# Combine weights in later slots, dispatched sums behind the last scores, another order of the last pairs, and the output rests of two batches in one transfer

## The chip, the cores and the metric

One core of a Trainium2 chip runs the kernel. Its engines work side by side: TensorE (PE; its weight loads are shown apart as PEld), VectorE (DVE), ScalarE (ACT), GpSimd (POOL), and SyncE (SP), which here only issues DMA transfers. Sixteen DMA engines move data between HBM and the on-chip memory. The metric is the device time of one execution in microseconds; the median of three runs before the change is 213.12 us.

## The reference

Inputs are `q`, `k`, `v` of shape [8 batches, 8 heads, 576, 64], and `phi` [512, 32], `w1` [8, 512, 1024], `w2` [8, 1024, 512].

```python
scores = (1/8) * q @ k.T                       # per batch and head
scores = where((i - j >= 0) & (i - j < 64), scores, -1e9)
attn   = softmax(scores) @ v                   # -> x: [4608, 512]
logits = x @ phi                               # [4608, 32]
d = softmax(logits, over the 4608 rows)        # dispatch
slot_input = d.T @ x                           # 32 slots, 4 for each of 8 experts
slot_out[e] = relu(slot_input[e] @ w1[e]) @ w2[e]
c = softmax(logits, over the 32 slots)         # combine weights
out = c @ slot_out                             # [4608, 512] in fp32
```

The dispatch softmax runs over all rows, so no output row can be made before the last row of x is known.

## The kernel before

Work goes by pairs of heads: 8 batches x 4 pairs = 32 pairs. The loop `for n in range(-1, NP)` (L492) is a software pipeline written out by hand: slot `n` issues stages of several pairs, and each engine runs its instructions in the order written. In slot n, PE transposes q of pair n and k of pair n+1 (L250), ScalarE copies them (`qb` L262, `kT` L257); PE computes the masked scores of pair n-1 for the row maxima (`st_max`, L273 and L276, in `a_m`), VectorE takes the maxima (L278, L289); PE computes the scores of pair n-2 (L299, L301; blocks 0 to 7 in `a_s`, the last block in `a_k`), ScalarE the exponentials (`pt`, L306, and L312 for the last block); PE multiplies pair n-3 with v (L323, in `a_v`), VectorE normalises it (L332, L333, into `x_b`); PE transposes pair n-4 (L347) and ScalarE copies it (`xt`, L351). L293 and L294 bring the maxima into the score matmul of the next pair.

Once for every batch, that is in every fourth slot each, stages of the mixture follow, with lags from the batch's first pair: at lag 8 the logits (`fr_logits`, L361, copied by ScalarE to `lg`, L366), at lag 9 the running maximum (`fr_max`, L371 and L373, `nmax`), its exponential (`fr_exp`, L387 and L388, `d` and `al`) and a 32x32 turn of the logits (`fr_turn`, L378, `lgT`), at lag 10 the dispatch (`fr_dispatch`, L433 and L434, copied to `dT`, L438 and L439) and the dispatched sums (`fr_slots`, L445 and L448, in `a_m`; added up by VectorE in `fr_acc`, L457). The combine weights are made at lag 11 (`cb_max`, L399), lag 12 (`cb_sub` on GpSimd L404, `cb_exp` on ScalarE L410, `cb_sum` on VectorE L416 and L417), lag 13 (`cb_mul` on GpSimd, L424) and lag 15 (`cb_turn` on VectorE, L429, into `ct_all`). The tiles `lg` and `ec` share one tag with two buffers.

GpSimd issues all loads of q, k, v and of the expert weights in `loads(n)` at the head of a slot. `w` are seven experts' weights, 1 MB a transfer; the eighth expert's come in quarters (`w1h` L125, `w2h` L131) into buffers of q and k. The last load is the fourth `w1h`, issued at L569 (`loads(NP)`).

Behind the loop L568 to L658 write out the last pairs and the last batch: the last scores, normalisations, transposes and logits, the merge of the maxima (`mg`), the dispatched sums, the normalised slot input `sit` (L643, L647). `fill(k)` issues k matmuls whose results nobody reads. Then `first` (L682) and `second` (L702) compute the experts with all 32 slots in four column groups, `osb` and `so4` carry the slot outputs, and the output loop (L730) makes for each batch 576 rows: 128-row blocks in pieces of one or two, and a rest of 64 rows. PE multiplies (L738), ScalarE and VectorE take turns to copy a piece to `ob` (four buffers of 5 x 512), and SyncE issues one transfer per piece (L748), 25 in all. Eight completion semaphores are used in turn for the transfers, so the issue of one waits for the one eight before it.

Of the kernel before, what the change touches and what calls it, by code (L numbers as in the profile page):

```python
# [9 lines left out]
FP32 = mybir.dt.float32  # L10
# [8 lines left out]
def kernel(  # L19
# [10 lines left out]
    nc = tc.nc  # L30
# [432 lines left out]
    def of(n, lag):  # L463
        b, r = divmod(n - lag, HP)
        return b if r == 0 and 0 <= b < B else None
# [26 lines left out]
    for n in range(-1, NP):  # L492
        loads(n)
        lb, eb, sb, cb = [of(n, lag) for lag in range(8, 12)]
        if of(n, 12) is not None:
            cb_sub(of(n, 12), nc.gpsimd)
        if of(n, 13) is not None:
            cb_mul(of(n, 13), nc.gpsimd)

        if live(n - 1):  # L500
            st_max(n - 1)
            st_max8(n - 1)
        if live(n - 3):
            st_av(n - 3)
        if live(n - 1):
            st_max8_read(n - 1)
        if live(n - 3):
            st_norm(n - 3)

        if live(n):  # L510
            st_transpose(n, "qs", a_qh)
            st_copy_q(n)

        if sb is not None:
            fr_dispatch(sb)
# [12 lines left out]
        if live(n + 1):  # L528
            st_transpose(n + 1, "ks", a_kh)
        if live(n - 2):  # L530
            st_exp8(n - 2)
        if live(n + 1):
            st_copy_k(n + 1)
        if eb is not None:
            fr_exp(eb)

        if lb is not None:
            fr_logits(lb)
        if live(n - 4):
# [23 lines left out]
    def fill(k):  # L563
        for _ in range(k):
            nc.tensor.matmul(a_k[:, :], ident_h[:, :], wm[:, 0:4, :].rearrange("p c x -> p (c x)"),
                             start=True, stop=True, skip_group_check=True)

    b, p = B - 1, NP - 1  # L568
# [22 lines left out]
    nc.vector.memset(a_s[:, 0, 128:192], -1.0e30)  # L591
# [6 lines left out]
    st_av(p)  # L598
    fr_stat(b - 1)
    st_norm(p)  # L600
# [5 lines left out]
    fr_dispatch_copy(b - 1, th, nc.vector.tensor_copy)  # L606
# [47 lines left out]
    cb_max(b)  # L654
    cb_sub(b, nc.vector)
    cb_sum(b - 1)
    cb_mul(b - 1, nc.vector)
    cb_turn(b - 1)  # L658
    pmid.close()
    patt.close()  # L660
    pex = ExitStack()
    psh = pex.enter_context(tc.tile_pool(name="psh", bufs=6, space=bass.MemoryType.PSUM))
# [3 lines left out]
        t = psh.tile([128, 512], FP32, name=name, tag="ph")  # L666
        return t, t[:, :].bitcast(FP16)

    ptl = ctx.enter_context(tc.tile_pool(name="ptl", bufs=1))
    pou = ctx.enter_context(tc.tile_pool(name="pou", bufs=4))  # L670


    so_ps = pso.tile([128, D], FP32, name="so_ps")
    op = pso.tile([128, D], FP32, name="op")
    hs = [ptl.tile([128, F], FP16, name=f"hs{g}") for g in range(2)]
    hT = [ptl.tile([128, NFC, 128], FP16, name=f"hT{g}") for g in range(2)]

    def first(g, f2):
        ha, _ = bank("ha")
# [19 lines left out]
    def second(g, fcs):  # L699
        for fc in fcs:  # L700
            for j in range(4):
# [17 lines left out]
    osb = ptl.tile([128, D], FP16, name="osb")  # L719
    nc.scalar.copy(out=osb, in_=op[:, :])  # L720
    nc.tensor.matmul(so_ps[:, :], ss[:, :, :].rearrange("p t s -> p (t s)"), osb[:, :], start=True, stop=True,
                     skip_group_check=True)
    so4 = ptl.tile([128, D], FP16, name="so4")
    nc.vector.tensor_copy(out=so4, in_=so_ps)
    pex.close()
    pst = ctx.enter_context(tc.tile_pool(name="pst", bufs=4, space=bass.MemoryType.PSUM))


    turn = 0
    for b in range(B):  # L730
        ob = pou.tile([128, 5, D], FP32, name="ob", tag="ob")
        for ts in ((0,), (1,), (2, 3), (4,)) if b == 0 else ((0, 1), (2, 3), (4,)):
            cp = pst.tile([128, 2, 512], FP32, name="cp", tag="cp")
            for i, t in enumerate(ts):
                pn = 128 if t < 4 else 64
                r = slice(32 * t, 32 * t + 32) if t < 4 else slice(96, 128)
                o = 0 if t < 4 else 128
                nc.tensor.matmul(cp[0:pn, i, :], ct_all[r, b, o:o + pn], so4[r, :], start=True, stop=True,  # L738
                                 skip_group_check=True)
            t0, nt = ts[0], len(ts)  # L740
            dst, src = ob[0:pn, t0:t0 + nt, :], cp[0:pn, 0:nt, :]
# [5 lines left out]
            r0 = 576 * b + 128 * t0  # L747
            nc.sync.dma_start(out=out[r0:r0 + pn * nt, :].rearrange("(c p) d -> p c d", p=pn), in_=dst)  # L748
# [1 line left out]
_INS = ['q', 'k', 'v', 'moe_phi', 'moe_w1', 'moe_w2']  # L750
_OUTS = [((4608, 512), 'float32')]
# [25 lines left out]
```

## Time and profile before

| | |
|---|---|
| median of 3 runs | 213.12 us (212.01 to 214.09) |
| the profiled execution | 211.88 us, its span 209.9 us |
| PE, DVE, ACT, POOL busy | 79%, 67%, 67%, 48% of the span |
| loop of 32 slots | to about 150 us |
| last pairs to `sit` | 150 to 168 us |
| experts (L682 to L724) | 168.3 to 179.1 us |
| output: first issue, last issue ended, end of span | 180.25, 205.27, 209.9 us |
| loads (q0) / output and phi (q1) | 30.94 MB / 9.50 MB |
| transfers of the output | 15 of 512 KB, 2 of 256 KB, 8 of 128 KB |

The span is the profiled stretch on the core; the execution's time includes 1.95 us around it. A line of the timeline gives start and length in us, engine, source line, operation, the tile written and the tiles read, the shape, and in brackets how long the engine was idle just before and what ended that. A DMA row gives the mean busy share of the 16 engines in tenths for each of 40 equal slices, and below it the rate in GB/s.

### The profile page before, as it was taken

How to read it: one execution, taken by the hardware profiler on the slowest of the kernel's cores; microseconds unless marked ns; L12 is line 12 of the kernel's file. 1: busy time of each engine (PE TensorE's matmuls, PEld its weight loads, DVE VectorE, ACT ScalarE, POOL GpSimd, SP SyncE). 2: the span in 40 equal slices, each digit the busy share in tenths (PEclk: the TensorE clock that was granted, in tenths of full speed). 3: DMA queues.
4: the chain of work that ended last, by engine and by line, in shares of the span. 5: the costliest groups of instructions: out<-in, count | busy, mean ns of one | idle time of the engine just before them, and what ended most of it. 6: DMA issues, size and time to landing. Idle time of an engine off the chain costs nothing.

```text
span 209.9 us, 6705 instructions
## 1 busy us (share of the span) xinstructions
PE 165.9 (79%) x2884; PEld 115.8 (55%) x2884; DVE 140.2 (67%) x332; ACT 140.0 (67%) x253; POOL 101.5 (48%) x122
## 2 busy tenths in 40 slices
PE   0696899998997999899899979989886898685000
PEld 0475677776776677577668857766673343211000
DVE  6888757667659685876869496677757574865200
ACT  2466687888888789878877987887665242744200
POOL 7969559284866476476828546653920000000000
PEclk9999999999999999999999999999999789955555
DMA  5999999999999999999999999999999910599996
GB/s 73 178 181 199 207 181 201 193 204 191 187 209 187 211 185 192 207 189 204 185 195 196 191 197 120 159 199 135 177 207 210 207 27 3 186 327 367 356 347 215
DMA packets 68124, 40.85 MB, mean 195 GB/s; under 512 B 38912, under 2 KB 59392, under 8 KB 68096
## 3 DMA queue, kind: packets, MB, share of 16 engines
q0 software_dynamic: 62560, 30.94, 111.3%
q1 hardware_dynamic: 5536, 9.50, 13.2%
q8 instruction: 22, 0.36, 0.6%
q14 instruction: 6, 0.05, 0.1%
HBM read 61.93 MB, written 9.44 MB: 340 GB/s over the span
## 4 chain that ended last, share of the span: by engine, by line
ACT 33%; PE 31%; DVE 18%; DMA 7%; issue 5%; SPq 0%; ACTq 0%; POOL 0%; DVEq 0%; POOLq 0%
ACT qb L262 10%; ACT pt L306 9%; DVE m L278 7%; DMA out_dram<-ob 4%; ACT xt L351 4%; PE a_m L273 4%; ACT kT L257 4%; PE a_q L250 4%; DVE x_b L333 4%; PE a_m L276 4%; ACT ob L743 3%; DMA qs<-in_q_dram 3%; PE ha L682 2%; PE a_v L323 2%; PE op L702 2%
## 5 line engine op out<-in xcount | busy, mean ns | idle before, releaser
L262 ACT ACTIVATE qb<-a_q 64x576 f16<-64x576 f16 x64 | 41.3, 645 | 22.5 <-PE a_q L250 22.0
L278 DVE TENSOR_REDUCE m<-a_m 128x8 f16<-128x1024 f32 x32 | 39.2, 1224 | 10.3 <-PE a_m L276 9.7
L306 ACT ACTIVATE pt<-a_s 128x1024 f16<-128x1024 f32 x32 | 32.8, 1024 | 3.1 <-PE a_s L301 2.3
L333 DVE TENSOR_TENSOR x_b<-a_v,rc 128x640 f16<-128x640 f32 x31 | 25.6, 824 | 1.1
L257 ACT ACTIVATE kT<-a_k 128x576 f16<-128x576 f16 x32 | 20.9, 654 | 5.0 <-PE a_k L250 5.0
L276 PEld LDWEIGHTS <-qb 128*128 128x128 f16 x256 | 17.1, 99 | 8.4 <-ACT qb L262 1.3
L79 POOL DMA_DIRECT2D ks<-in_k_dram x16 | 11.1, 692 | 20.9 <-PE a_k L250 18.1
L147 POOL DMA_DIRECT2D v<-in_v_dram x16 | 19.9, 1241 | 2.5 <-DMA ks<-in_k_dram 2.1
L351 ACT COPY xt<-a_q 128x576 f16<-128x576 f16 x31 | 20.2, 651 | 0.8 <-PE a_q L347 0.8
L276 PE MATMUL a_m<-kT,qb 128*128 128x128 f16 x256 | 20.0, 222 | 0.0
L250 PE MATMUL a_k<-ident_h,ks 96*64 96x96 f16 x384 | 15.0, 217 | 6.3 <-DMA ks<-in_k_dram 6.3
L299 PE MATMUL a_s<-rt,lh 128*128 128x128 f16 x256 | 19.8, 220 | 0.1
L273 PE MATMUL a_m<-wm,ident_h 128*128 128x512 f16 x64 | 19.8, 392 | 0.0
L154 POOL COPY v<-v 64x1152 f16<-64x1152 f16 x16 | 18.3, 1142 | 2.6 <-DMA v<-in_v_dram 2.0
L301 PE MATMUL a_s<-qb,kT 128*128 128x128 f16 x256 | 19.5, 219 | 0.0
L294 DVE CAST rt<-a_v 9x128 f16<-9x128 f32 x31 | 9.0, 289 | 15.8 <-PE a_v L293 15.6
L299 PEld LDWEIGHTS <-lh 128*128 128x128 f16 x288 | 17.6, 98 | 3.3 <-issue 1.6
L301 PEld LDWEIGHTS <-kT 128*128 128x128 f16 x288 | 18.8, 98 | 0.0
L156 POOL COPY v<-v 64x1088 f16<-64x1088 f16 (+1 forms) x16 | 17.9, 1117 | 0.8
L250 PE MATMUL a_q<-ident_h,qs 96*64 96x96 f16 x384 | 15.0, 212 | 3.3 <-ACT xt L351 0.9
L743 ACT COPY ob<-cp 128x1024 f32<-128x1024 f32 (+2 forms) x13 | 10.5, 848 | 8.6 <-DMA out_dram<-ob 6.5
L323 PE MATMUL a_v<-v,pt 128*64 128x65 f16 x558 | 15.7, 197 | 0.6 <-ACT pt L306 0.6
(144 smaller groups left out, 305.8 us busy)
## 6 DMA issues: line engine op xcount, KB each, us to landing
w<-in_moe_w_dram POOLq DMA_DIRECT2D x14, 1024.0 KB, 15.6
out_dram<-ob SPq DMA_DIRECT2D x15, 512.0 KB, 4.6
ks<-in_k_dram POOLq DMA_DIRECT2D x16, 288.0 KB, 12.6
qs<-in_q_dram POOLq DMA_DIRECT2D x16, 288.0 KB, 14.1
v<-in_v_dram POOLq DMA_DIRECT2D x16, 288.0 KB, 13.8
w2h<-in_moe_w_dram POOLq DMA_DIRECT2D x4, 256.0 KB, 7.2
w1h<-in_moe_w_dram POOLq DMA_DIRECT2D x4, 256.0 KB, 10.8
out_dram<-ob SPq DMA_DIRECT2D x8, 128.0 KB, 4.5
```

The lines of the kernel that those rows point to most:

```text
L147: nc.gpsimd.dma_start(out=v1s[b % 2][:, c, 0:Dh], in_=v[b].rearrange("h s d -> (h s) d").rearrange("(c p) d -> p c d", p=128)[:, c, :])
L250: nc.tensor.transpose(tq[64 * hf:64 * hf + 64, RP * r:RP * r + RP], src[0:RP, h + hf, Dh * r:Dh * r + Dh], ident_h[0:RP, 0:RP])
L257: nc.scalar.activation(kTs[p % NK][:, 64:64 + S], turned(a_kh), AF.Copy, scale=QKS)
L262: nc.scalar.activation(qbs[p % NQ][h, :, hf, :], turned(a_qh)[h], AF.Copy, scale=QKS)
L273: nc.tensor.matmul(a_m[:, j, :], ident_h[:, :], wm[:, j:j + 4, :].rearrange("p c x -> p (c x)"), start=True, stop=False, skip_group_check= ...
L276: nc.tensor.matmul(a_m[:, i // 4, 128 * (i % 4):128 * (i % 4) + 128], qblock(p, i), kwindow(p, i), start=False, stop=True, skip_group_chec ...
L278: nc.vector.reduce_max(m[:, 0:8].rearrange("p (l c) -> p l c", l=2), a_m[:, :, :].rearrange("p l (c x) -> p l c x", x=128), axis=AXX)
L299: nc.tensor.matmul(at(i), lh[:, i, :], rt[:, :], start=(i % 4 == 0), stop=False, skip_group_check=True)
L301: nc.tensor.matmul(at(i), kwindow(p, i), qblock(p, i), start=False, stop=True, skip_group_check=True)
L306: nc.scalar.activation(pt[:, 0:8, :].rearrange("p i x -> p (i x)"), a_s[:, :, :], AF.Exp, scale=XS)
L333: nc.vector.tensor_tensor(out=xbs[b][:, :, 128 * hp:128 * hp + 128].rearrange("p c (l d) -> p l c d", l=2), in0=avv[:, :, :, 0:64], in1=rc ...
L351: nc.scalar.copy(out=xts[b][:, hp, :], in_=a_qh[:, 0:S])
```

## The change

Four things are changed.

1. In the loop `cb_mul` goes from lag 13 to 17, `cb_exp` from 12 to 15, `cb_sum` from 12 to 16 and `cb_turn` from 15 to 19; `cb_sub` stays at 12.
2. In the loop the last block's scores (`st_scores(n - 2, (8,), ...)`) stand ahead of the dispatched sums `fr_acc(sb, fr_slots(sb))`.
3. Behind the loop, the maximum and the turn of batch 6 (`fr_max`, `fr_turn`) stand ahead of the normalisation of the last pairs, and the memset of `a_s` between these; the combine steps of the last batches are spread differently, most of them behind the experts' last VectorE operation; `fill` takes the bank it writes, and there are 4, 2, 5 and 2 of them (3, 2, 1, 4 and 1 before); the dispatched sums of the last batch stand ahead of the matmul that sums `ws`; `hs`, `hT`, `osb` use buffers of earlier tiles; `so4` is copied by ScalarE.
4. The output goes by two batches: four pieces of 128-row blocks (five for the first two batches) and one rest piece, in which 64 rows of each of two batches lie under each other on 128 partitions and go out in one transfer. `ob` has ten buffers of 2 x 512. There are 21 transfers. The sums, multiply and turn of the last batch stand ahead of the second two batches' pieces.

The core of the diff:

```diff
@@ the loop
-        if of(n, 13) is not None:
-            cb_mul(of(n, 13), nc.gpsimd)
+        if of(n, 17) is not None:
+            cb_mul(of(n, 17), nc.gpsimd)
...
+        if live(n - 2):
+            st_scores(n - 2, (8,), lambda i: s8)
         if sb is not None:
             fr_acc(sb, fr_slots(sb))
-        if live(n - 2):
-            st_scores(n - 2, (8,), lambda i: s8)
...
-        if of(n, 12) is not None:
-            cb_exp(of(n, 12))
+        if of(n, 15) is not None:
+            cb_exp(of(n, 15))
...
-        if of(n, 12) is not None:
-            cb_sum(of(n, 12))
-        if of(n, 15) is not None:
-            cb_turn(of(n, 15))
+        if of(n, 16) is not None:
+            cb_sum(of(n, 16))
+        if of(n, 19) is not None:
+            cb_turn(of(n, 19))
@@ behind the loop
-    cb_exp(b - 2)
-    cb_sum(b - 2)
-    cb_mul(b - 2, nc.gpsimd)
     st_score(p)
     st_scores(p, (8,), lambda i: s8)
     st_exp8(p)
+    fr_max(b - 1)
+    fr_turn(b - 1)
+    st_av(p - 1, a_m)
+    st_norm(p - 1, a_m)
     nc.vector.memset(a_s[:, 0, 128:192], -1.0e30)
-    st_av(p - 1, a_m)
-    fr_max(b - 1)
-    st_norm(p - 1, a_m)
...
     fr_transpose_copy(p, a_kh)
+    cb_sum(b - 3)
+    cb_mul(b - 3, nc.gpsimd)
...
-    fill(3)
+    fill(4, a_k[:, :])
...
-    fill(2)
...
     fr_dispatch_copy(b)
+    fill(2, a_m[:, 1, :])
...
-    fill(1)
+    fr_acc(b, fr_slots(b, a_v[:, 0, :]))
     nc.tensor.matmul(mg[:, 4:5], ssf_, ws[:, :], start=True, stop=True, skip_group_check=True)
-    fr_acc(b, fr_slots(b, a_v[:, 0, :]))
-    fill(4)
+    fill(5, a_m[:, 1, :])
...
-    fill(1)
+    fill(2, a_m[:, 1, :])
...
-    cb_turn(b - 2)
-    fr_turn(b - 1)
-    cb_max(b - 1)
-    cb_sub(b - 1, nc.vector)
-    cb_exp(b - 1)
     fr_turn(b)
     cb_max(b)
     cb_sub(b, nc.vector)
-    cb_sum(b - 1)
-    cb_mul(b - 1, nc.vector)
-    cb_turn(b - 1)
-    pmid.close()
+    cb_exp(b - 2)
...
     cb_exp(b)
-    cb_sum(b)
-    cb_mul(b, nc.vector)
-    cb_turn(b)
+    cb_max(b - 1)
+    cb_sub(b - 1, nc.vector)
+    cb_sum(b - 2)
+    cb_mul(b - 2, nc.vector)
+    cb_exp(b - 1)
+    cb_turn(b - 3)
+    cb_turn(b - 2)
+    cb_sum(b - 1)
+    cb_mul(b - 1, nc.vector)
+    cb_turn(b - 1)
     second(1, range(8))
...
-    nc.vector.tensor_copy(out=so4, in_=so_ps)
+    nc.scalar.copy(out=so4, in_=so_ps)
@@ the output
-    for b in range(B):
-        ob = pou.tile([128, 5, D], FP32, name="ob", tag="ob")
-        for ts in ((0,), (1,), (2, 3), (4,)) if b == 0 else ((0, 1), (2, 3), (4,)):
+    for b in range(0, B, 2):
+        pieces = [(b + i, ts) for i in range(2) for ts in ((0, 1), (2, 3))] + [(b, (4,))]
+        if b == 0:
+            pieces[0:1] = [(0, (0,)), (0, (1,))]
+        if b == 2:
+            cb_sum(B - 1)
+            cb_mul(B - 1, nc.vector)
+            cb_turn(B - 1)
+        for b_, ts in pieces:
...
+                    for j in range(2):
+                        nc.tensor.matmul(cp[64 * j:64 * j + 64, i, :], ct_all[96:128, b_ + j, 128:192],
+                                         so4[96:128, :], start=True, stop=True, skip_group_check=True)
...
+            if t0 < 4:
+                nc.sync.dma_start(out=out[r0:r0 + 128 * nt, :].rearrange("(c p) d -> p c d", p=128), in_=dst)
+            else:
+                nc.sync.dma_start(out=out[S * b_:S * b_ + 2 * S, :].rearrange("(t s) d -> t s d", t=2)[:, 512:S, :],
+                                  in_=ob[:, 0, :])
```

More of the change, by code (lines that the diff above doesn't have):

```diff
@@ L556, with fill @@
             cb_max(cb)
-        if of(n, 12) is not None:
-            cb_sum(of(n, 12))
-        if of(n, 15) is not None:
-            cb_turn(of(n, 15))
-    def fill(k):
+        if of(n, 16) is not None:
+            cb_sum(of(n, 16))
+        if of(n, 19) is not None:
+            cb_turn(of(n, 19))
+    def fill(k, bank):
         for _ in range(k):
-            nc.tensor.matmul(a_k[:, :], ident_h[:, :], wm[:, 0:4, :].rearrange("p c x -> p (c x)"),
+            nc.tensor.matmul(bank, ident_h[:, :], wm[:, 0:4, :].rearrange("p c x -> p (c x)"),
                              start=True, stop=True, skip_group_check=True)
@@ L598 @@
     st_av(p)
+    st_norm(p)
     fr_stat(b - 1)
-    st_norm(p)
     fr_transpose(p - 1)
@@ L605 @@
     fr_dispatch(b - 1, th)
-    fr_dispatch_copy(b - 1, th, nc.vector.tensor_copy)
+    fr_dispatch_copy(b - 1, th)
     fr_transpose(p, a_kh)
     fr_transpose_copy(p, a_kh)
+    cb_sum(b - 3)
+    cb_mul(b - 3, nc.gpsimd)
     fr_acc(b - 1, fr_slots(b - 1))
@@ L667, in bank @@
         return t, t[:, :].bitcast(FP16)
-    ptl = ctx.enter_context(tc.tile_pool(name="ptl", bufs=1))
-    pou = ctx.enter_context(tc.tile_pool(name="pou", bufs=4))
     so_ps = pso.tile([128, D], FP32, name="so_ps")
     op = pso.tile([128, D], FP32, name="op")
-    hs = [ptl.tile([128, F], FP16, name=f"hs{g}") for g in range(2)]
-    hT = [ptl.tile([128, NFC, 128], FP16, name=f"hT{g}") for g in range(2)]
+    hs_ = pxb.tile([128, 2, F], FP16, name="hs", tag="x_b")
+    hT_ = pxb.tile([128, 2, NFC, 128], FP16, name="hT", tag="x_b")
+    hs, hT = [hs_[:, g, :] for g in range(2)], [hT_[:, g, :, :] for g in range(2)]
     def first(g, f2):
@@ L714 @@
     cb_exp(b)
-    cb_sum(b)
-    cb_mul(b, nc.vector)
-    cb_turn(b)
+    cb_max(b - 1)
[8 more added lines that the diff above has]
+    cb_turn(b - 1)
     second(1, range(8))
-    osb = ptl.tile([128, D], FP16, name="osb")
+    osb = kTs[0][:, 0:D]
     nc.scalar.copy(out=osb, in_=op[:, :])
@@ L722 @@
                      skip_group_check=True)
+    pmid.close()
+    ptl = ctx.enter_context(tc.tile_pool(name="ptl", bufs=1))
+    pou = ctx.enter_context(tc.tile_pool(name="pou", bufs=10))
     so4 = ptl.tile([128, D], FP16, name="so4")
-    nc.vector.tensor_copy(out=so4, in_=so_ps)
+    nc.scalar.copy(out=so4, in_=so_ps)
     pex.close()
@@ L729 @@
     turn = 0
-    for b in range(B):
-        ob = pou.tile([128, 5, D], FP32, name="ob", tag="ob")
-        for ts in ((0,), (1,), (2, 3), (4,)) if b == 0 else ((0, 1), (2, 3), (4,)):
+    for b in range(0, B, 2):
[7 more added lines that the diff above has]
+        for b_, ts in pieces:
             cp = pst.tile([128, 2, 512], FP32, name="cp", tag="cp")
+            ob = pou.tile([128, 2, D], FP32, name="ob", tag="ob")
             for i, t in enumerate(ts):
[L735 to L739, printed above, removed]
+                if t < 4:
+                    r = slice(32 * t, 32 * t + 32)
+                    nc.tensor.matmul(cp[:, i, :], ct_all[r, b_, 0:128], so4[r, :], start=True, stop=True,
+                                     skip_group_check=True)
+                else:
+                    for j in range(2):
+                        nc.tensor.matmul(cp[64 * j:64 * j + 64, i, :], ct_all[96:128, b_ + j, 128:192],
+                                         so4[96:128, :], start=True, stop=True, skip_group_check=True)
             t0, nt = ts[0], len(ts)
-            dst, src = ob[0:pn, t0:t0 + nt, :], cp[0:pn, 0:nt, :]
+            dst, src = ob[:, 0:nt, :], cp[:, 0:nt, :]
             if turn % 2 == 0:
@@ L746 @@
             turn += 1
-            r0 = 576 * b + 128 * t0
-            nc.sync.dma_start(out=out[r0:r0 + pn * nt, :].rearrange("(c p) d -> p c d", p=pn), in_=dst)
+            r0 = S * b_ + 128 * t0
+            if t0 < 4:
+                nc.sync.dma_start(out=out[r0:r0 + 128 * nt, :].rearrange("(c p) d -> p c d", p=128), in_=dst)
+            else:
+                nc.sync.dma_start(out=out[S * b_:S * b_ + 2 * S, :].rearrange("(t s) d -> t s d", t=2)[:, 512:S, :],
+                                  in_=ob[:, 0, :])
 _INS = ['q', 'k', 'v', 'moe_phi', 'moe_w1', 'moe_w2']
```

## The prediction

> **What bounds the kernel now.** I read the page's slices first, then the output stage by its DMA rates, then the loop and the way out of it by the timeline.
>
> ```profile
> DMA  5999999999999999999999999999999910599996
> GB/s 73 178 181 199 207 181 201 193 204 191 187 209 187 211 185 192 207 189 204 185 195 196 191 197 120 159 199 135 177 207 210 207 27 3 186 327 367 356 347 215
> ```
>
> Each slice is 5.25 us. Loads fill the DMA engines to slice 31, apart from slices 24, 25 and 27, which miss (80 + 41 + 65 GB/s) x 5.25 us = 0.98 MB of a 200 GB/s rate: 4.8 us of loading. From 178 us the output fills them again. The DMA view of 180 to 209 us alone, in slices of 0.725 us:
>
> ```profile
> DMA  0499998999999999999999999999999999999920
> GB/s 0 181 367 381 384 263 201 401 404 393 271 333 404 401 348 274 401 404 393 266 328 407 401 356 268 390 404 390 288 328 390 401 376 243 384 398 404 299 93 0
> ...
> q1 hardware_dynamic: 5008, 9.44, 94.3%
> ```
>
> The engines never idle, so this stage lasts as long as its bytes take. Full rate is about 395 GB/s, 24.7 per engine: a row of 2,048 bytes takes 83 ns. Eight times the rate falls to 200 to 290 with the engines still busy: these are the eight rests, 64 rows from 64 partitions each. The stage is 4,608 rows / 16 engines = 288 rows x 83 ns = 23.9 us, plus eight rests at about half rate, 8 x 0.33 = 2.6 us: 26.5 us, against about 27.2 seen (181.1 to 208.3).
>
> The loop, one batch of four slots (18.8 us), from the timeline:
>
> ```profile
> 107.24 0.40 PE L445 MATMUL a_m<-x_b,dT 128*32 128x512 f16 x4 [0.24 <-DVE dT L438]
> ...
> 108.59 0.28 ACT L312 ACTIVATE pt<-a_k 128x128 f16<-128x128 f32 x1 [0.49 <-PE a_k L250]
> ...
> 110.92 1.30 ACT L262 ACTIVATE qb<-a_q 64x576 f16<-64x576 f16 x2 [0.98 <-PE a_q L250]
> ...
> 118.71 0.41 ACT L410 ACTIVATE ec<-lgT 128x192 f32<-128x192 f32 x1
> ...
> 119.15 0.35 DVE L416 TENSOR_REDUCE rs<-ec 128x6 f32<-128x192 f32 x1 [1.35 <-ACT ec L410]
> ...
> 119.76 1.23 DVE L278 TENSOR_REDUCE m<-a_m 128x8 f16<-128x1024 f32 x1
> ...
> 122.22 0.22 PE L293 MATMUL a_v<-ident_h,m 128*9 128x128 f16 x1 [0.99 <-DVE x_b L333]
> ...
> 122.77 0.46 ACT L387 ACTIVATE d<-lg,nmax 128x192 f16<-128x192 f32 x1 [0.31 <-DVE nmax L373]
> ```
>
> VectorE waits 1.35 us for the combine exponential; the row maxima (L278) queue behind it, then the normalisation, PE's L293 and nmax. The way out of the loop, and the last load:
>
> ```profile
> 149.79 0.58 POOL L125 DMA_DIRECT2D w1h<-in_moe_w_dram  x1
> ...
> 157.20 0.11 DVE L591 MEMSET a_s<- 128x64 f32 x1 [0.46 <-ACT pt L306]
> ...
> 159.21 0.82 DVE L333 TENSOR_TENSOR x_b<-a_v,rc 128x640 f16<-128x640 f32 x1
> ...
> 165.89 0.75 DVE L457 SCALAR_TENSOR_TENSOR acc<-acc,al,a_v 128x512 f32<-128x512 f32 x1 [1.12 <-PE a_v L448]
> ```
>
> That w1h landing is the slowest of its kind, 20.4 us: 170.2. Its matmul (L682) starts at 171.09, so the load is 0.9 us from being the bound.
>
> **The change, part by part.** Times in the frame of the 211.88 us execution (span 209.9).
>
> *Combine weights later (loop).* In its new slot the exponential stands behind xt, where ACT waits 0.53 us for PE's q transposes before qb (115.04) and the exponential takes 0.41: hidden. Its old place was such a gap too (xt 118.18, qb 119.39, both 1.2 us apart as in a slot without it), so ACT gains nothing directly. VectorE does the sums at about 117.85 without a wait, L278 starts when its matmuls end (118.5 instead of 119.76), nmax is ready at 121.45, and d follows kT at 122.34, not 122.77: 0.43 us less until the next qb. The multiply on POOL moves four slots; its 1.05 us wait for the sums goes, and loads queued behind it (w1h, 120.41) go no later. The exponential takes a buffer whose readers ended slots before: no new wait.
>
> *Dispatched sums behind the last scores.* PE's L445 waits for dT, which stands behind L333. With L333 1.0 us earlier (L293 no longer held up 0.99) dT is ready first. PE then runs scores, last scores (0.2 us), sums, and the ks transposes start at 126.07 where they had 126.91 (108.10 one batch on): 0.84 earlier, 0.41 of it beyond the 0.43. The last exponential no longer waits 0.49. PE's chain to the q transposes behind qb (0.98 idle) is that much shorter. Per batch 0.85 us, for the five batches that have the stall: 4.25; without VectorE's stall the reorder alone is worth about 0.2.
>
> *Order of the last pairs.* nb, nmax and lgT no longer queue behind the memset, which waits for pt at 157.20; the first normalisation goes from 158.04 to 156.9, the second from 159.21 to 158.07, the last logits, limited then by dT and the sums on VectorE, come 0.97 us earlier. Two fills leave the path in front of the dispatch (0.25), and the sums go ahead of L633, which waited for ws: acc at 164.86 on the old scale, 1.03 earlier. Together 2.0 us. Fills are 13 instead of 11; at 0.21 us they fit, but at the half clock of 165.8 to 169.2 five take 2.1 us where 1.3 is free: up to 0.8 us back.
>
> *The load behind it.* The gain of 2.0 passes the slack of 0.9, and the loads must move too. They can follow the loop at most 4.8 us (the holes above); I take 3.8 of 4.25, since holes fill one by one. So the start of the w1h matmul moves 3.8 + 0.9 - 0.05, and the 1.1 us left of the tail's gain is a PE wait, which also covers the extra fills. After it VectorE, free of ct_all's turns, has hs ready (0.25), and so4 on ACT takes 0.59 instead of 0.69 (0.1). First output 5.0 us earlier; bounds 2 and 7.5.
> The turns moved to VectorE's end are 11 operations at 0.34 us from 175.05: 178.8, and the first ob copy, which now waits for them because ob lies where they read, had 179.59: 0.8 us of cover. The last batch's sums (1.3 us) stand among output copies, where VectorE idles 6.3 us.
>
> *Rests of two batches in one transfer.* 25 output transfers become 21. Each transfer so far is one list of 64, 96 or 128 rows (or partitions) outermost on both sides. The new one has 128 partitions on one side and two batches outermost on the other. How such a pair is divided among 16 engines no row shows. Two ends: (a) like the others, 8 rows to each of 16 engines, from all partitions, which takes the half rate away: -2.6 us; (b) one batch to an engine, two engines, since two equal shares are all that the outermost counts 2 and 128 have in common. Then the busiest engine has 256 rows of the pieces plus 4 x 64 of rests, 512 x 83 ns = 42.5 us, against 26.5: +16.0. In general 256 + 512/k rows for k engines: k = 4 costs 31.9 us, about the 5.0 gained. Other engines cannot help: the completion of eight transfers back gates each issue, and every eight hold a rest. I take (b): every division seen so far is of the outermost counts as they stand (64 and 128 into 16).
> [...] The trace agrees as far as it goes: 5,536 packets less 4,608 rows and 512 of phi are 416, 16 completions for each of 26 transfers, all with outermost counts that 16 divides.
> [...]
>
> Sum: 211.88 - 5.0 + 16.0 = 222.9 us. The profiled execution lies 1.24 below the median of 213.12.
>
> **Rivals.**
> Rests spread over all engines (a), the other sign: 211.88 - 5.0 - 2.6 = 204.3. For it: the dips cost 2.6 us and 128 partitions show none. Against: the two outermost batches. Chance 0.14.
> Two engines, and no early gain: the loads stay where they are because the queue is full, or VectorE stalls elsewhere. For it: DMA at 9 tenths throughout. Against: the holes. 211.88 - 1 + 16.0 = 226.9. Chance 0.10.
> Some middle number of engines: 4 to 8, 26.9 to 31.9 us for the stage, 207 to 212. Chance 0.04.
>
> **How the numbers follow.** The forecast keeps 0.72. A row takes 81 ns on an engine at the highest rate (404 GB/s); two engines nearly alone may be quicker, and I allow 76. The mean over the stage, its half-rate rests included, is 27.2 x 16 / 4,608 = 94 ns; with four rests that reach all partitions I stop at 90. That gives 38.9 to 46.1 us for the stage, +12.4 to +19.6; with early gains of 7.5 to 1 the slow cases span 216.8 to 230.5. I give 216 to 229, which leaves out the spread case and little more. About 1% is what can be told from no change. Slower: 0.72 + 0.10 = 0.82, and 0.01 of the middle; faster 0.15; same 0.02.
>
> **What would show it.** (b): from the second pair of batches on, the DMA share in the output stage falls to a few tenths at 50 to 250 GB/s, the last transfers land long after their issue, and ob copies wait for DMA. (a): no dips, stage of about 24 us. Loop: L416 without a wait, 18.0 us per batch. Load: L682 waits for DMA w1h about 1 us. The forecast is wrong if the output stage keeps near 400 GB/s to its end.

## The result, and the profile after

The changed kernel takes 223.85 us (median of four runs, 222.33 to 224.72) where the kernel before, run beside it, takes 213.39 us (212.01 to 214.09): a ratio of 1.049, 95% interval 1.041 to 1.058. It is slower, by 10.5 us of medians. The forecast was 222.9 us in a range of 216 to 229. The profiled execution of the changed kernel is one of 224.72 us with a span of 222.9, against 211.88 and 209.9 before: 13.0 us longer.

The slices of the page, now 5.57 us each:

```profile
DMA  5999999999999999999999999999970099593910
GB/s 66 179 179 205 195 185 205 188 211 187 196 196 202 190 189 207 192 203 183 198 193 203 190 188 203 172 191 207 208 123 3 0 374 324 185 295 127 300 50 38
```

The holes at slices 24, 25 and 27 of the page before have shrunk to one small one (172): the loads now keep up with a faster loop, at the same 200 GB/s. The new thing stands at the end. Counted from 0, the output begins at slice 32, and from slice 34 on the DMA engines are no longer full: shares of 5, 9, 3, 9, 1, 0. The DMA view of 174 to 222 us alone, in slices of 1.2 us:

```profile
DMA  0003999999999611799999111799999211111110
GB/s 0 0 0 137 379 369 384 367 360 348 297 295 340 251 55 50 271 350 285 285 290 333 70 49 51 236 259 304 275 311 376 102 51 51 51 50 51 51 51 31
...
q1 hardware_dynamic: 4888, 9.44, 58.1%
```

The bytes are the 9.44 MB of before, but the engines spend 58% of the stretch on them instead of 94%. Three times the rate falls to about 50 GB/s, the last time for some ten microseconds. The windows view gives the share of busy engines beside the rate (columns: stretch, its length, granted clock, DMA share, GB/s):

```profile
core 0: us, , PEclk, DMA share, GB/s
...
212.00:214.00 2.00, 0.50 0.13 51
214.00:218.00 4.00, 0.50 0.13 51
218.00:221.00 3.00, 0.50 0.13 51
```

A share of 0.13 is 2 of 16 engines; 51 GB/s are 25.5 for each, so a row of 2,048 bytes takes 80 ns. The packets of the queue say the same by count: 5,416, less 4,608 rows and 512 of phi, leaves 296 completions. Eighteen transfers (17 pieces and phi) with 16 each are 288; the other four, the joint rests, posted two each. The waits view shows who pays:

```profile
ACT ob L752 <- DMA out_dram<-ob: 14.4, 4, 6.2
...
DVE ob L754 <- DMA out_dram<-ob: 8.6, 3, 5.4
...
PE ha L671 <- DMA w1h<-in_moe_w_dram: 2.5, 1, 2.5
```

(us in total, times, longest). The output copies wait up to 6.2 us for a buffer that a transfer still reads. From the first output issue to the end of the span it is 45.4 us (177.51 to 222.9) where it was 29.65 (180.25 to 209.9): 15.7 us more. The first output itself goes out 2.74 us earlier. 15.7 - 2.7 = 13.0, the difference of the spans.

The loop, from the timeline (start, us, engine, line; in brackets a wait ahead of it):

```profile
90.45 1.30 ACT L262 ACTIVATE qb<-a_q 64x576 f16<-64x576 f16 x2 [0.98 <-PE a_q L250]
...
97.37 0.35 DVE L416 TENSOR_REDUCE rs<-ec 128x6 f32<-128x192 f32 x1
98.03 1.23 DVE L278 TENSOR_REDUCE m<-a_m 128x8 f16<-128x1024 f32 x1
...
104.96 0.40 PE L445 MATMUL a_m<-x_b,dT 128*32 128x512 f16 x4
105.60 0.31 PEld L250 LDWEIGHTS <-ks 96*64 96x64 f16 x12 [0.23 <-issue]
...
108.42 1.30 ACT L262 ACTIVATE qb<-a_q 64x576 f16<-64x576 f16 x2 [0.98 <-PE a_q L250]
```

L416 waits for nothing now (1.35 us before), L445 neither, and the batch from qb to qb takes 17.97 us instead of 18.81. The way to the first output, from the timeline and then by windows:

```profile
145.59 0.58 POOL L125 DMA_DIRECT2D w1h<-in_moe_w_dram  x1
...
167.09 0.38 PE L671 MATMUL ha<-w1h,sit 128*32 128x512 f16 x1 [2.50 <-DMA w1h<-in_moe_w_dram]
...
168.69 0.63 PE L671 MATMUL ha<-w1h,sit 128*32 128x512 f16 x1
169.10 1.93 PE L691 MATMUL op<-w,hT 128*32 128x512 f16 x16
```

```profile
core 0: us, PE busy (x), PEclk, DMA share, GB/s
168.00:169.00 1.00, 1.00 (x17) 0.76 0.00 0
169.00:170.00 1.00, 1.00 (x16) 0.50 0.06 16
170.00:171.00 1.00, 1.00 (x13) 0.50 0.00 0
171.00:172.00 1.00, 1.00 (x16) 0.54 0.00 0
172.00:173.00 1.00, 1.00 (x21) 1.00 0.00 0
```

PE waits 2.5 us for the last w1h, and then the granted clock is half for some 3.4 us, just while the expert matmuls run: the sixteen of L691 take 1.93 us; the same sixteen take 1.04 at full clock in the interleaved kernel below. Before, a like stretch of half clock lay at 165.8 to 169.2, on the way out of the loop.

### The profile page after: what moved, and what is told of

Same layout as the page of the kernel before. It is cut to its first block, busy times and chain, and to the rows that moved or that the text cites. A ratio compares the mean times of both kernels' runs of the same rounds, so it can differ in the third digit from the quotient of the medians.

```text
span 222.9 us, 6682 instructions
## 1 busy us (share of the span) xinstructions
PE 162.9 (73%) x2886; PEld 115.9 (52%) x2886; DVE 138.0 (62%) x330; ACT 138.7 (62%) x252; POOL 100.8 (45%) x121
## 3 DMA queue, kind: packets, MB, share of 16 engines
q1 hardware_dynamic: 5416, 9.50, 12.7%
HBM read 61.93 MB, written 9.44 MB: 320 GB/s over the span
## 4 chain that ended last, share of the span: by engine, by line
PE 33%; ACT 26%; DMA 18%; DVE 7%; issue 3%; POOL 1%; SPq 1%; ACTq 0%; POOLq 0%
DMA w1h<-in_moe_w_dram 10%; ACT qb L262 9%; DMA out_dram<-ob 6%; ACT pt L306 6%; PE a_q L250 5%; ACT kT L257 4%; ACT xt L351 4%; PE a_m L273 3%; PE a_s L299 3%; PE a_m L276 3%; DMA qs<-in_q_dram 3%; DVE ob L754 3%; PE a_s L301 2%; PE a_v L323 2%; PE a_k L250 2%
## 5 line engine op out<-in xcount | busy, mean ns | idle before, releaser
L752 ACT COPY ob<-cp 128x1024 f32<-128x1024 f32 (+1 forms) x11 | 9.4, 910 | 15.8 <-DMA out_dram<-ob 14.4
L250 PEld LDWEIGHTS <-qs 96*64 96x64 f16 x384 | 12.8, 111 | 8.1 <-issue 7.0
```

What stands on the lines that cost most here:

```text
L250: nc.tensor.transpose(tq[64 * hf:64 * hf + 64, RP * r:RP * r + RP], src[0:RP, h + hf, Dh * r:Dh * r + Dh], ident_h[0:RP, 0:RP])
```

## The experiments

The kernel before was run beside each group and had medians of 213.1 to 214.9 us, so comparisons between groups are made by the ratios, at 213.4 us to 1.

**Are the joint rests the whole loss?** First the changed kernel with each joint rest as two transfers, one per batch:

```diff
-                nc.sync.dma_start(out=out[S * b_:S * b_ + 2 * S, :].rearrange("(t s) d -> t s d", t=2)[:, 512:S, :],
-                                  in_=ob[:, 0, :])
+                for j in range(2):
+                    r0 = S * (b_ + j) + 512
+                    nc.sync.dma_start(out=out[r0:r0 + 64, :], in_=ob[64 * j:64 * j + 64, 0, :])
```

> The changed kernel with each rest transfer cut in two, 64 rows of one batch from 64 partitions each (25 transfers again, all with rows outermost). Theory (two engines carry the joint rests): the output stage falls from 45.4 us (first issue to the end of the span) to the 29.7 us of before, time 223.9 - 15.7 = 208.1 us, and no stretch at 50 GB/s. Rival (the stage is long because of the ten small buffers, or because the last batch's combine steps stand among the copies): stays above 220 us.

Measured: 207.43 us, ratio 0.970 (0.963 to 0.976). The same rows in the same places, and 16.4 us less, with more transfers (25) than the changed kernel has. In its profile no stretch of the output falls to 50 GB/s before the last slice, and the completions are 416, 16 for each of 26 transfers. (The profiled execution is the longest of the four, 210.99 us.)

The other way round, the kernel before with nothing of the change but its output loop (and its ten buffers):

```diff
-    for b in range(B):
-        ob = pou.tile([128, 5, D], FP32, name="ob", tag="ob")
+    for b in range(0, B, 2):
...
+                nc.sync.dma_start(out=out[S * b_:S * b_ + 2 * S, :].rearrange("(t s) d -> t s d", t=2)[:, 512:S, :],
+                                  in_=ob[:, 0, :])
```

> The kernel before with the changed output loop alone (pairs of batches, joint rests, ten small buffers), nothing else changed. Theory: +15.7 us, 229.1 us. Rival (the joint rests hurt only together with the earlier start or the combine steps in the output stage): below 220 us.

Measured: 229.39 us, ratio 1.075 (1.070 to 1.081), 15.9 us over before. The 296 completions are there, and so is the tail at 50 GB/s: its DMA view of 180 to 229 us reads

```profile
DMA  0003999999999511999993114998994111111100
GB/s 0 0 0 142 378 375 381 375 346 338 276 301 356 206 52 59 366 351 313 294 328 140 52 52 157 281 301 251 279 381 186 50 52 52 48 47 52 50 38 0
```

Its stage is 45.4 us as well (183.57 to 229.0); its first output is late in this execution, for the granted clock was half from 159.9 to 173.6 us, so the time is taken from the medians. The two edits agree: the joint transfer costs 16 us, and all else in the change gains about 5.5 (229.39 to 223.85).

**Is it the list, not the joining?** The rests stay joined, but the two batches are interleaved on the partitions, by four small copies on POOL, so that 64 rows are outermost on the side of HBM:

```diff
+        nc.gpsimd.tensor_copy(out=ctr[96:128, b // 2, :, :],
+                              in_=ct_all[96:128, b:b + 2, 128:192].rearrange("p t s -> p s t"))
...
-                    for j in range(2):
-                        nc.tensor.matmul(cp[64 * j:64 * j + 64, i, :], ct_all[96:128, b_ + j, 128:192],
+                    nc.tensor.matmul(cp[:, i, :], ctr[96:128, b_ // 2, :, :].rearrange("p s t -> p (s t)"),
...
-                nc.sync.dma_start(out=out[S * b_:S * b_ + 2 * S, :].rearrange("(t s) d -> t s d", t=2)[:, 512:S, :],
+                nc.sync.dma_start(out=out[S * b_:S * b_ + 2 * S, :].rearrange("(t s) d -> s t d", t=2)[512:S, :, :],
```

> The changed kernel with the rests of two batches interleaved on the partitions (GpSimd copies the weights' columns into that order), so that the joint transfer has 64 rows outermost in HBM and 2 batches inside, from all 128 partitions. Theory: 16 engines carry it and no half-rate dips remain: 2.6 us below the kernel with the rests apart, 205.5 us; stage about 27 us, all rates near 400 GB/s, 16 completions for each transfer. Rival (the dips of before come from the rests' rows in HBM and not from 64 partitions): the dips stay, 208 us.

Measured: 204.56 us, ratio 0.960 (0.956 to 0.964). Its DMA view of 175 to 202 us:

```profile
DMA  0799999999999999999999999999999999999910
GB/s 0 267 376 379 376 388 370 379 373 379 385 382 385 352 385 388 382 385 352 388 382 388 370 379 385 364 410 349 388 370 388 364 376 388 385 388 385 388 55 0
...
q1 hardware_dynamic: 4944, 9.44, 94.7%
```

No dip is left, neither to 50 nor to the 200 to 290 of before. The same rows of HBM are written, so the eight dips of before did not come from where the rests lie in HBM. Completions are 352 = 22 x 16, the stage 27.3 us from first issue to end. This is end (a) of the prediction's two (204.3 us): the same bytes, the same 128 partitions, the same number of transfers. What was changed is the order of the rows in the list, and with it the partition that each row lies on.

**Four equal shares.** The changed kernel with rests of four batches with 32 rows each, the batch outermost (four on the side of HBM, 128 partitions on the other), two such transfers behind every fourth batch:

```diff
-        pieces = [(b + i, ts) for i in range(2) for ts in ((0, 1), (2, 3))] + [(b, (4,))]
+        pieces = [(b + i, ts) for i in range(2) for ts in ((0, 1), (2, 3))]
+        if b % 4 == 2:
+            pieces += [(b - 2, (4,)), (b - 2, (5,))]
...
-                nc.sync.dma_start(out=out[S * b_:S * b_ + 2 * S, :].rearrange("(t s) d -> t s d", t=2)[:, 512:S, :],
+                c0 = 128 * t0 if t0 == 4 else 544
+                nc.sync.dma_start(out=out[S * b_:S * b_ + 4 * S, :].rearrange("(t s) d -> t s d", t=4)[:, c0:c0 + 32, :],
```

> The changed kernel with rests of four batches in one transfer, 32 rows of each, four batches outermost in HBM; four such transfers of 128 rows as before. Theory (the outermost count sets the engines): four engines, the busiest with 256 + 4 x 32 = 384 rows instead of 512, 10.6 us less: 213.3 us, four completions for each rest, stretches at about 100 GB/s. Rival (any joint transfer of several batches runs on two engines, or its rows are slow by themselves): 222 to 226 us.

Measured: 218.37 us, ratio 1.024 (1.018 to 1.031). The count is as expected, 304 = 18 x 16 + 4 x 4, four engines; the time is not: five microseconds over. The windows of its end show where they are lost:

```profile
core 0: us, , PEclk, DMA share, GB/s
...
203.00:205.00 2.00, 0.50 0.40 151
205.00:207.00 2.00, 0.50 0.26 44
207.00:209.00 2.00, 0.50 0.22 53
209.00:211.00 2.00, 0.50 0.26 85
211.00:213.00 2.00, 0.50 0.16 58
```

From 205 to 209 some four engines are busy (0.24 x 16), at 12 GB/s each on average: half of what an engine moves in the changed kernel when only two are left. Two more runs were made to see whether that is the late issue or the rows themselves. In the first, an edit of the four-batch kernel, the four transfers go behind the pieces of batches 0 to 3:

```diff
-        if b % 4 == 2:
-            pieces += [(b - 2, (4,)), (b - 2, (5,))]
+        if b < 4:
+            pieces[2:2] = [(2 * b, (4,))]
+            pieces += [(2 * b, (5,))]
```

> The kernel with the rests of four batches in one transfer, with these four transfers issued earlier: behind the pieces of batches 0, 1, 2 and 3 instead of two at a time behind batches 3 and 7. It took 218.37 us where 213.3 was expected, and its four busy engines moved 48 GB/s in all from 205 to 209 us, 12 each, where two engines move 25 each in the changed kernel. Theory A, the late issue makes it: with early rests the busiest engine's 256 + 128 rows x 80 ns = 30.7 us run without a hole and the time falls to 207 to 209 us. Theory B, an engine that takes 32 rows from 32 neighbouring partitions runs at half rate: 256 x 80 + 128 x 160 ns = 41 us, 217 to 219 us, nothing gained. Between them both have a part.

Measured: 216.74 us, ratio 1.016 (1.007 to 1.025). That is far from theory A's 207 to 209, so the late issue is not the whole. Whether it has a part the times do not tell, for the interval reaches theory B's 217 to 219 and overlaps that of the four batches (1.018 to 1.031); in the profiles the stage is 37.9 us instead of 40.7. In the second, an edit of the interleaved kernel, eight batches with 16 rows each, batch outermost again:

```diff
-        nc.gpsimd.tensor_copy(out=ctr[96:128, b // 2, :, :],
-                              in_=ct_all[96:128, b:b + 2, 128:192].rearrange("p t s -> p s t"))
+            for g in range(4):
+                nc.gpsimd.tensor_copy(out=ctr[96:128, g, :, :],
+                                      in_=ct_all[96:128, :, 128 + 16 * g:144 + 16 * g])
...
+                nc.sync.dma_start(out=out.rearrange("(t s) d -> t s d", t=B)[:, 512 + 16 * b_:528 + 16 * b_, :],
```

> The kernel with the rests interleaved, with another interleaving: each rest transfer takes 16 rows of all eight batches, the batch outermost (eight equal shares, 128 partitions), four such transfers behind the pieces of batches 2, 3, 4 and 5. By the rule that the outermost count is divided among the engines, eight engines get 16 rows each: 8 x 4 completions for the rests, 320 packets in all for completions, and the busiest engine has 256 + 64 = 320 rows x 80 ns = 25.6 us, about the 27.3 us that the stage takes with 16 engines: 204.5 to 206 us. If engines that take rows from few neighbouring partitions run at half rate (theory B of the four batches), 256 x 80 + 64 x 160 ns = 30.7 us: 208 us. Rival: only the last dimension or the bytes count and all 16 engines share it: 352 completions and 204.5 us.

Measured: 211.36 us, ratio 0.992 (0.989 to 0.995). The count is again that of the outermost dimension, 320 = 18 x 16 + 4 x 8, so in all three divisions tried (two, four, eight) the completions of a rest are as many as its outermost count; the time is 3 to 7 us over what each theory said. Set beside each other, with the stage from the first output issue to the end of the span, and the rows of the busiest engine at the 83 ns of the prediction:

| kernel | engines for a rest | rows on the busiest | x 83 ns | stage | rest of the stage |
|---|---|---|---|---|---|
| interleaved | 16 | 288 | 23.9 | 27.3 | 3.4 |
| eight batches | 8 | 320 | 26.6 | 33.6 | 7.0 |
| four batches, early | 4 | 384 | 31.9 | 37.9 | 6.0 |
| four batches | 4 | 384 | 31.9 | 40.7 | 8.8 |
| the change | 2 | 512 | 42.5 | 45.4 | 2.9 |

Rows alone leave 2.9 and 3.4 us at the two ends and 6 to 9 between. The packet records of the traces, which hold the start and length of every row's transfer, show how the time goes. It is not that all rows are slow, as theory B has it: of the 95 rows that the four-batch kernel starts from 205 to 209 us the median takes 84 ns, as everywhere, but 12 take over 300 ns and one 1,113. Over the whole output no row takes more than 135 ns in the interleaved kernel, while 49 take over 300 in the changed one, 47 and 62 with four batches (late and early) and 23 with eight.

One explanation, the author's guess from the rates of four engines (48 GB/s in all) and of two (51), was tried with the last run: that partitions 32 apart share a way out of SBUF, so that engines in step on them halve each other. The changed kernel's joint rest is cut into two transfers of 2 x 32 rows, with the rows of the two batches 32 partitions apart:

```diff
-                nc.sync.dma_start(out=out[S * b_:S * b_ + 2 * S, :].rearrange("(t s) d -> t s d", t=2)[:, 512:S, :],
-                                  in_=ob[:, 0, :])
+                for h in range(2):
+                    c0 = 512 + 32 * h
+                    nc.sync.dma_start(
+                        out=out[S * b_:S * b_ + 2 * S, :].rearrange("(t s) d -> t s d", t=2)[:, c0:c0 + 32, :],
+                        in_=ob[64 * h:64 * h + 64, 0, :])
```

> The changed kernel with each joint rest of 128 rows cut into two transfers of 2 x 32 rows, on partitions 0 to 63 and 64 to 127: the same rows on the same two engines, but the two engines now walk partitions that lie 32 apart instead of 64. Theory, partitions 32 apart share a way out of SBUF: four engines that walk partitions s, 32+s, 64+s, 96+s moved 48 GB/s in all (two pairs at 24), two that walk s and 64+s moved 51. Then these two move about 24 GB/s in all, a rest row takes 169 ns instead of 80 to 91, 256 of them per engine add 20 to 23 us to 223.85: 240 to 248 us, and the stretches in which only two engines work show 24 to 27 GB/s instead of 51. Rival: the slow rate of the four and eight engines came from the other side, rows 1.18 MB apart in HBM, or from the number of rows; then two batches in lock step move 51 GB/s as before and the time is 223.9 us, at most 1 us more for four further issues. [...]

Measured: 225.59 us, ratio 1.053 (1.048 to 1.058), and the windows of its end:

```profile
core 0: us, , PEclk, DMA share, GB/s
...
212.00:214.00 2.00, 0.50 0.13 51
214.00:218.00 4.00, 0.50 0.13 47
218.00:221.00 3.00, 0.50 0.08 31
```

Two engines still move 47 to 51 GB/s. The theory fails for two engines as it was put: no 20 us, but 0.8 us by ratio, and a stage of 47.2 us (175.13 to 222.3), 1.8 more than the changed kernel's. Theory B fails with it: if an engine takes the rows of one batch, as the counts have it, here too each takes 32 rows from 32 neighbouring partitions, and each moves about 25 GB/s. That two engines 32 partitions apart slip out of step by a few partitions and four or eight cannot is a way to keep it, and no run tested that. The other candidate, rows that go to four or eight places in HBM at once, was not tested either. What makes four and eight engines slower than their rows stays open.

**What the early part of the change gains, and what limits it.** Four kernels start from the interleaved one. In the first, the last w2 transfer is issued behind the last w1h instead of ahead of it:

```diff
-    WSLOTS[NP - 1] = [11, 12, 13]
+    WSLOTS[NP - 1] = [11, 12]
+    WSLOTS[NP] = [13]
```

> The kernel with the rests interleaved, with one edit: the last w2 transfer is issued behind the last w1h instead of ahead of it. The theory that the last w1h limits the early gain: in the kernel with the rests interleaved PE still waited 1.43 us for w1h, and in the changed kernel 2.5 us and then ran at half clock. With one load less ahead of it w1h lands some 5 us earlier, that wait goes, the first output comes 1.0 to 1.5 us earlier (about 173.7) and the time is about 203.2 us. Rival 1: the wait turns into one for the last w2, of about the same length, and the time stays at 204.5. Rival 2: w1h was not the bound, another wait of the way out takes its place and less than 0.3 us is gained.

Measured: 202.49 us (six runs, 202.21 to 203.18), ratio 0.947 (0.943 to 0.950). The last w1h's first use and the first output in the interleaved kernel, then in this one:

```profile
166.18 0.38 PE L671 MATMUL ha<-w1h,sit 128*32 128x512 f16 x1 [1.43 <-DMA w1h<-in_moe_w_dram]
...
175.01 3.14 SPq L760 DMA_DIRECT2D out_dram<-ob  x5
```

```profile
144.83 0.57 POOL L125 DMA_DIRECT2D w1h<-in_moe_w_dram  x1
147.73 0.89 POOL L116 DMA_DIRECT2D w<-in_moe_w_dram  x1
...
164.31 0.38 PE L672 MATMUL ha<-w1h,sit 128*32 128x512 f16 x1
...
173.14 3.14 SPq L761 DMA_DIRECT2D out_dram<-ob  x5
```

The wait is gone, no wait for w2 takes its place, and the first output is 1.87 us earlier, more than the 1.0 to 1.5 expected. The order of two loads was the bound of the early part, and this kernel is faster than both that were compared.

The second puts the combine weights back at their old lags (12, 12, 13, 15); the three steps of batch 4 behind the loop, which the late lags had left there, go with it:

> The kernel with the rests interleaved, with the combine weights back at their old slots in the loop (exponential and sums 12 slots behind, multiply 13, turn 15). The step of the prediction: VectorE's 1.35 us wait comes back in each batch, the period returns to about 18.6 to 18.8 us, five batches, so the loop ends 3.2 to 4.2 us later; the loads move with it by at least 3.2 us and PE's wait for w1h (1.43 us) takes up to 1.4 of it: 3.0 to 4.0 us more, 207.5 to 208.5. Rival: the reorder of the sums carries most of the 0.85 us per batch, then the lags are worth 2 us or less: under 206.5.

Measured: 208.85 us, ratio 0.976 (0.972 to 0.980). VectorE's wait is back:

```profile
100.14 0.41 ACT L410 ACTIVATE ec<-lgT 128x192 f32<-128x192 f32 x1
...
100.58 0.35 DVE L416 TENSOR_REDUCE rs<-ec 128x6 f32<-128x192 f32 x1 [1.34 <-ACT ec L410]
```

The third puts the dispatched sums ahead of the last scores again:

```diff
-        if live(n - 2):
-            st_scores(n - 2, (8,), lambda i: s8)
         if sb is not None:
             fr_acc(sb, fr_slots(sb))
+        if live(n - 2):
+            st_scores(n - 2, (8,), lambda i: s8)
```

> The kernel with the rests interleaved, with the dispatched sums ahead of the last scores again. The step of the prediction: of 0.85 us per batch 0.43 comes by VectorE and 0.41 by PE's order, so the period is 18.4 us instead of 17.97, five batches 2.1 us; PE's wait for w1h hides up to 1.4 of it if the loads do not move: 0.7 to 2.1 us more, 205.3 to 206.6. Rival 1: with VectorE's stall gone dT is ready before PE gets there in either order, the order is worth under 0.1 us per batch and the time stays at 204.6.

Measured: 205.21 us, ratio 0.959 (0.955 to 0.963), that of the interleaved kernel (0.960); in its profile the first output is 0.7 us later. The fourth undoes both:

> The kernel with the rests interleaved, with both edits of the loop undone; the order of the last pairs stays. Period 18.8 us as before, the loop ends 4.2 us later, the tail keeps its 2.0 us, w1h lands about 170 and is not waited for by more than 1.5 us: first output about 3.2 to 4.0 us later than with them, 207.8 to 208.6. If the two edits add up, the difference to 204.56 is the sum of those of the two runs that undo one each; if the order gains only where the stall is gone, undoing the order on top of the lags costs 0.2 us per batch or less.

Measured: 207.96 us, ratio 0.972 (0.969 to 0.976). The four by their timelines:

| loop | batch, qb to qb | ks transposes behind qb | PE's wait for w1h | first output |
|---|---|---|---|---|
| both edits (interleaved) | 17.98 | 1.94 | 1.43 | 175.01 |
| order undone | 18.07 | 2.05 | 1.56 | 175.73 |
| lags undone | 18.87 | 2.42 | 0.90 | 178.88 |
| both undone | 18.82 | 2.36 | 1.19 | 178.61 |

The lags carry the loop's gain, 0.75 us of 0.84 per batch; the order is worth 0.09 beside them, and without them nothing (18.87 against 18.82). The two do not add up.

Last, the kernel before with only its output loop replaced by the interleaved one, which leaves the order of the last pairs as it was:

> The kernel before with nothing changed but its output loop, which is that of the kernel with the rests interleaved: loop order, combine lags and the order of the last pairs are as before. First output at 180.25 us as before, the stage 27.3 us instead of 29.65, since the eight dips go: 2.4 us faster than before, about 211.0 us (ratio 0.989). Beside the kernel with both loop edits undone (ratio 0.972) it gives what the order of the last pairs is worth behind the load: first outputs 180.25 against 178.61, 1.6 us, by the profiles; the prediction has 0.9 there, since the loads would not move with the tail alone. Rival 1: the dips cost nothing, 213.4. Rival 2: the tail order is worth its whole 2.0 us or more, then 210 or less cannot be.

Measured: 211.43 us, ratio 0.991 (0.986 to 0.996): the eight dips cost 1.9 us of the 2.4 expected, within the interval. Its first output goes at 181.11, in the kernel with both loop edits undone at 178.61. So what the change does between the loop and the output (the order of the last pairs, the fills, so4 on ScalarE) is worth 2.5 us by the profiles and 4.0 +- 1.3 by the ratios, against the 1.6 expected of that run. Part of it may be the clock: it is half from 160.1 to 163.6 us in this profile, and full until 181.7 in the other.

## Why the prediction was right, and where it was not

**The division among engines** was the deciding step, taken between two ends, and it holds: two completions for each joint rest, two engines at 25.5 GB/s. Every other division that ran went by the outermost counts too: 4 and 8 completions for counts of 4 and 8 against 128 (304 and 320 in all), and 16 for 64 (352). Rival (a) was a real alternative, but of another list: the interleaved kernel's 204.56 us is its 204.3.

**The price of it**, 512 rows x 83 ns less the 26.5 us of before = 16.0 us, is measured at 15.7 by the profiles and 15.9 by the output loop alone. The bounds of 76 and 90 ns hold the row (80 alone). For eight engines the prediction's own formula gives 26.6 us where it has 26.9. The half rate of the 64-row rests was sized at 2.6 us; removing it alone gave 1.9 by the ratio and 2.35 by the stage (29.65 to 27.3). Rests of 64 rows from 64 partitions show the dips (200 to 290 GB/s), joint rests from 128 partitions in the interleaved kernel do not (349 and more between its first and its last slices); what slows the former no run shows. With the two batches' rows 32 partitions apart two engines show no half rate (47 to 51 GB/s).

**The loop** was forecast at 18.0 us per batch and ran at 17.97; the last qb came 4.19 us earlier (148.54 to 144.35) for the 4.25 of the sum. What failed inside it is the split: "0.84 earlier, 0.41 of it beyond the 0.43" was put down to PE's order. With the lags alone the transposes already follow qb by 2.05 us instead of 2.36, since L445's dT is ready in either order; the order adds 0.1. The "about 0.2" for the order without the stall was too much as well.

**The order of the last pairs** was sized at 2.0 us. `sit` is ready at 161.36 instead of 167.81, 6.45 earlier; without the loop's 4.19 that is 2.26. Part of it is the clock and not the order: four fills ahead of `sit` took 1.89 us at half clock in the kernel before, five took 1.24 in the changed one. The 0.8 us feared for the fills at half clock were not due: the clock was full from 160 to 168 us.

**The load behind it** is the term that was off in the profiled execution: first output 2.74 us earlier instead of 5.0. "They can follow the loop at most 4.8 us; I take 3.8": w1h landed at 167.0 instead of 170.2, 3.2 us earlier, and PE waited 2.50 us instead of 1.1. Then 1.6 us went to the half clock: from w1h's first matmul to the first output it took 10.42 us, where the interleaved kernel, with the same instructions on that path, took 8.83 (and the kernel before 9.16, so that the 0.35 for VectorE and so4 held: 0.33). The interleaved kernel's w1h came 0.9 us sooner and its first output at 175.01, 5.24 us earlier than before. Six kernels have this early part (the changed one, the interleaved one, and those with four, four early and eight batches and with 32 rows); their first outputs go at 174.81 to 177.51 us, in the middle at 175.3, which is 4.9 earlier than before, and the changed kernel's is the latest. So the shortfall belongs to one execution more than to the sum: by the medians of the output loop alone and of the whole change, all else gained 5.5 us. That the load would be the bound behind the tail was right, and the load's order decided it.

**The cover** that was named for the turns at VectorE's end held: they end at 175.8, and the first ob copy comes at 176.9. The sums of the last batch among the output copies cost nothing that shows; there VectorE idles as forecast.

The total agreed with the median, 222.9 against 223.85, for the stated reasons; with the profiled execution (224.72) it was 1.8 us short, of which the load and the clock are 2.3 and the stage -0.3. As a difference it was forecast at 11.0 us and came out at 10.5 by the medians and 12.8 by the profiled executions.

## What to carry to other kernels

Read a transfer's two lists before joining transfers: in every division tried here the outermost counts of both sides decided how many engines share it (2, 4, 8 and 16 by their completions, for 2, 4, 8 and 64 against 128), and the completions in the queue's packet count told it from the trace (296, 304, 320 and 352); where a joint list would start with 2, interleave the rows, as here, where 64 came first and the stage fell from 45.4 to 27.3 us. Price an uneven transfer by the rows of its busiest engine, and do not trust that sum between the ends, where it fell 3 to 6 us short here. When a compute chain is made shorter, look at which load lands last on its new path and in what order the loads are issued: here swapping two gained 1.9 us, nearly as much as the reordering of a whole tail.

## What was not expected of the hardware

- Four engines that alone carried 32 rows each of two rests moved 48 GB/s in all (12 each), while two engines moved 51 (25 each), with the two batches' rows 64 partitions apart, and 47 to 51 with 32. The median row took 84 ns in both cases; with four, single rows took up to 1.1 us. The cause stays open.
- While a joint rest is under way together with other pieces, all engines read as busy (0.98) at 295 GB/s, not at the 380 of the interleaved kernel, in the changed kernel at 196 to 200 us. Two stalled engines of 16 would leave 14/16 x 380 = 332 GB/s, so engines that have no part in the rest are slower too.
- A stretch of half granted clock falls near the end of the compute part at a place that differs between executions: 165.8 to 169.2 us in the kernel before, 168.5 to 171.9 in the changed one, 159.9 to 173.6 in the output loop alone, 160.1 to 163.6 in the kernel before with the interleaved output loop. On PE's path it cost 1.6 us in the changed kernel's profile. All three profiles with the old order of the last pairs have such a stretch. With the new order it comes with the longest waits of PE for w1h: the changed kernel (2.50 us) has it, and so has the kernel with the rests apart (2.84 us of waiting, half clock from 167.9 us), while the other nine, with waits of 0 to 2.41 us, keep the full clock to 175.9 us or later. So the length of the wait may decide it; no run tested that.
